# Two phases of attention scores cut anew, with one query tile's scores in the output banks and the division ahead of the minima

## The chip, the cores and the metric

The kernel runs on one core of one Trainium2 chip. The metric is the device time of one execution in microseconds (us). Three runs of the kernel before took 685.50, 690.76 and 686.28 us, so the median is 686.28 us; one more, profiled execution took 683.86 us.

## The reference

A windowed attention over 8 batches and 8 heads is followed by a mixture of experts. Only the attention is touched by the change.

```python
B, H, S, D = (8, 8, 576, 64); window = 128
scores = scale * q @ k^T
mask = (rel >= 0) & (rel < window)          # rel = query position - key position
scores = where(mask, scores + slope[h] * -abs(rel), -1e9)
attn = exp(scores - max(scores)); attn = attn / (sum(attn) + 1e-9)
x = attn @ v                                # then x becomes 4608 tokens of 512
logits = x @ w_gate                         # each expert takes the 576 best tokens left
out[mask_e] = relu(x[mask_e] @ w1[e]) @ w2[e]
```

## The kernel before

**The work of a pair.** Two heads of one batch make a pair, so there are 32 pairs. A query tile `t` holds 128 queries, two blocks of 64, of one head (`t` = 0 to 3), and a fifth half tile holds the remaining block of both heads. Which block remains depends on the parity of the batch: in even batches `t` = 0 has 2 key blocks and `t` = 4 has 3, in odd batches `t` = 0 has 3 and `t` = 4 has 1; tiles 1 to 3 always have 3. A key block is 64 columns wide. All of it is in fp32 on 64x64 quadrants of TensorE (PE), four products at a time: two heads by two query blocks.

**The steps of a pair**, each on one engine:

- `scores` (PE, through `mm`, L54): products of queries and keys into two banks `s`, one for each head, of 512 columns.
- `least` (VectorE, DVE, L134): bias and score are added, and the smallest value of each row goes to `mn`. Tiles 0 to 3 take one instruction for each head, the half tile takes two.
- `exps` (ScalarE, ACT, L145): the exponential, with the row's sum.
- `turn` (PE, L158 and L54): the weights are transposed into banks `pt`; `turned` (L166) copies them out, tiles 2 and 0 on ACT, tiles 1 and 3 on DVE.
- `av` (PE): products of values and weights into two banks `x`; `copy_out` (ACT, L214) copies them to `xT`.
- `natural` (PE): `xT` is transposed back and multiplied by the gate's weights, into two `pt` banks `N`.
- `divide` (DVE, L240 to L255): the reciprocal of the row sums, then the gate's part `Lp` and the output `xb` of both `N` banks are multiplied by it; `store` sends `xb` out on the DMA queue of SP.

**Banks.** PSUM has eight banks: `ps_s` has 2, `ps_t` (tiles `pt`) has 4 and `ps_x` has 2. `scores` is called twice for a pair, with `UNITS = (2, 3), (0, 1, 4)` (L23), and takes two tiles of `ps_s` each time, so the second half can be written only when the minima of the first half have read the same two banks.

**The order.** The loop over `n` (L316) writes the work of several pairs into one pass, and `put` (L51) keeps each engine to the order in which the code is written. In a pass the order is: `copy_out` of pair n-4, `least` of pair n-1's second half, `turn` of pair n-2's tiles 2, 1 and 3, `exps` of the second half, the copies of `pt`, `natural` of pair n-4, `turn` of tiles 0 and 4, at most one step of the router's early work on DVE (`router.early_step`), `scores`, `least` and `exps` of pair n's first half, `divide` of pair n-4, `av` of pair n-3, and `scores` of pair n's second half. Each of these engines runs its own instructions in that order and waits where another has not come so far.

## Time and profile before

| what | value |
|---|---|
| median of 3 runs | 686.28 us (685.50 to 690.76) |
| the profiled execution | 683.86 us, span 681.7 us |
| PE busy | 655.0 us, 96% of the span |
| DVE busy | 468.5 us, 69% |
| ACT busy | 386.4 us, 57% |
| attention's passes with scores | to about 204 us of the span |
| routing and experts | the rest of the span |

The profile lists, for each group of instructions, its busy time, the mean of one and the idle time of the engine ahead of them with what ended it. A busy PE is not a PE at its peak: the ends of products are modelled, and a product that overlaps others counts as busy. The timeline gives the start of each instruction or run of equal instructions in us, its length, the engine, the line and the tiles, and in brackets the idle time ahead of it. The engines wait for one another through semaphores.

### The profile page before, as it was taken

The numbers are of one execution on the slowest core, as the hardware profiler recorded it, in microseconds if no ns is written. First come the engines' busy times: TensorE is split into PE (matmuls) and PEld (weight loads), VectorE is DVE, ScalarE is ACT, GpSimd is POOL, SyncE is SP. The second block draws the span as 40 slices with busy tenths as digits, with TensorE's granted clock in tenths as the row PEclk, the third lists the DMA queues.
The fourth block names the chain that finished last, engine by engine and source line by source line (L and its number), as shares of the span: only waits on it lengthen the run. The fifth ranks groups of instructions, "written<-read, shape, count | busy, mean of one in ns | idle before, by whom it ended". The sixth has DMA issues, their size and how long they took to land.

```text
span 681.7 us, 18901 instructions
## 1 busy us (share of the span) xinstructions
PE 655.0 (96%) x7152; PEld 580.3 (85%) x7152; DVE 468.5 (69%) x1985; ACT 386.4 (57%) x1091; POOL 134.2 (20%) x296
## 2 busy tenths in 40 slices
PE   7999999999996699999999999999999999999995
PEld 4998998998986399889779879989989989989985
DVE  5788888888887799979749879776756625423210
ACT  6998898898884162434224546455546645644210
POOL 4021121121121201421412124013014014011011
PEclk9999999999998699999999999999999999999999
DMA  8556566566532361814515736637546556421001
GB/s 304 155 180 203 180 181 205 178 185 201 179 101 76 99 220 53 295 39 155 178 47 198 191 115 214 130 100 228 111 116 201 137 119 201 124 70 39 1 25 50
DMA packets 58980, 98.65 MB, mean 145 GB/s; under 512 B 27648, under 2 KB 36992, under 8 KB 58880
## 3 DMA queue, kind: packets, MB, share of 16 engines
q1 hardware_dynamic: 52992, 78.48, 38.6%
q0 software_dynamic: 5888, 18.88, 8.4%
q8 instruction: 58, 0.95, 0.6%
q14 instruction: 42, 0.34, 0.2%
HBM read 72.57 MB, written 18.87 MB: 134 GB/s over the span
## 4 chain that ended last, share of the span: by engine, by line
PE 86%; DVE 8%; DMA 3%; issue 1%; ACT 1%; POOL 0%; SPq 0%; POOLq 0%; DVEq 0%; ACTq 0%
PE ph L1059 24%; PE po L1087 10%; PE po L1088 10%; PE s L54 9%; PE po L1090 8%; PE pt L54 7%; PE pt L158 7%; PE x L54 6%; DMA raw<-in_w_dram 2%; DVE hl L967 2%; DVE hlo L1069 1%; PE m L610 1%; DVE u L134 1%; PE pg L1000 1%; PE ph L984 1%
## 5 line engine op out<-in xcount | busy, mean ns | idle before, releaser
L1059 PE MATMUL ph<-xh,hl 128*128 128x288 f32 (+2 forms) x1024 | 188.3, 298 | 0.6 <-ACT hh L1064 0.5
L1059 PEld LDWEIGHTS ph<-xh,hl 128*128 128x128 f32 x1024 | 154.6, 189 | 2.1 <-ACT hh L1064 0.7
L145 ACT ACTIVATE u<-u,mn 128x192 f32<-128x192 f32 (+2 forms) x288 | 123.9, 433 | 24.5 <-DVE mn L134 24.5
L1087 PE MATMUL po<-hl,hh 128*128 128x512 f32 (+1 forms) x328 | 128.3, 391 | 0.0
L1088 PE MATMUL po<-hl,hh 128*128 128x512 f32 (+1 forms) x328 | 126.2, 385 | 0.0
L1059 PE MATMUL ph<-xl,hl 128*128 128x288 f32 (+2 forms) x512 | 115.5, 297 | 0.0
L134 DVE CUSTOM_DVE_ANT_0 u<-s,bm 128x192 f32<-128x192 f32 x308 | 86.5, 333 | 30.0 <-PE s L54 29.2
L1064 ACT ACTIVATE hh<-ph 128x288 fp32r<-128x288 f32 (+2 forms) x128 | 46.5, 408 | 106.3 <-PE ph L1059 103.1
L1090 PE MATMUL po<-hl,hlo 128*128 128x512 f32 (+1 forms) x264 | 101.3, 384 | 0.0
L967 DVE TENSOR_TENSOR hl<-raw,hl 128x512 fp32r<-128x512 f32 x128 | 85.1, 684 | 22.0 <-ACT hl L965 21.6
L1099 POOL DMA_INDIRECT out_dram<-o,idx x40 | 42.2, 1056 | 274.9 <-ACT o L1094 216.0
L1059 PEld LDWEIGHTS ph<-xl,hl 128*128 128x128 f32 x512 | 84.1, 189 | 0.2 <-DVE xl L1038 0.2
L965 ACT CAST hl<-raw 128x1024 fp32r<-128x1024 f32 x64 | 65.9, 1051 | 22.1 <-DMA raw<-in_w_dram 17.7
L54 PE MATMUL s<-qk 64*64 64x192 f32 (+1 forms) x1112 | 69.7, 319 | 1.9 <-DVE mn L134 1.6
L1069 DVE SCALAR_TENSOR_TENSOR hlo<-ph,hh 128x288 fp32r<-128x288 f32 (+2 forms) x128 | 49.1, 416 | 32.5 <-ACT hh L1064 31.9
L1087 PEld LDWEIGHTS po<-hl,hh 128*128 128x128 f32 x328 | 61.8, 188 | 11.2
L1088 PEld LDWEIGHTS po<-hl,hh 128*128 128x128 f32 x328 | 61.7, 188 | 11.3
L1094 ACT COPY o<-po 128x512 f32<-128x512 f32 (+1 forms) x33 | 18.9, 573 | 91.0 <-PE po L1090 80.8
L1090 PEld LDWEIGHTS po<-hl,hlo 128*128 128x128 f32 x264 | 49.7, 188 | 9.9
L158 PE MATMUL pt<-ident_sb,u 128*128 128x128 f32 x368 | 54.2, 282 | 1.4 <-DVE mn L134 1.0
L54 PEld LDWEIGHTS s<-qk 64*64 64x64 f32 x1112 | 48.3, 132 | 8.1 <-issue 2.5
L145 ACT ACTIVATION_READ_ACCUMULATOR u<-u,mn 128x1 f32 x288 | 54.4, 189 | 0.0
(240 smaller groups left out, 902.6 us busy)
## 6 DMA issues: line engine op xcount, KB each, us to landing
raw<-in_w_dram SPq DMA_DIRECT2D x64, 512.0 KB, 4.3
qk<-in_qk_dram SPq DMA_DIRECT2D x32, 576.0 KB, 5.1
v<-in_v_dram SPq DMA_DIRECT2D x32, 288.0 KB, 3.6
x<-xb SPq DMA_DIRECT2D x14, 512.0 KB, 3.5
x<-xb SPq DMA_DIRECT2D x8, 128.0 KB, 3.2
x<-xb SPq DMA_DIRECT2D x4, 256.0 KB, 2.3
g<-x,idx POOLq DMA_INDIRECT x40, 3.8
out_dram<-o,idx POOLq DMA_INDIRECT x40, 2.8
```

The source lines that it names most:

```text
L54: put(nc.tensor.matmul(out, w, a, start=start, stop=stop, skip_group_check=True))
L134: put(nc.vector.tensor_tensor_reduce(out=u[rows], in0=x[rows, c:c + 64 * m].rearrange("q (j k) -> q j k", k=64), in1=bm[n % NP][rows, y:y ...
L145: put(nc.scalar.activation(u, u, AF.Exp, bias=st["mn"][:, i:i + 1], scale=-1.0, accum_out=st["sm"][:, i:i + 1]))
L158: put(nc.tensor.transpose(ps[:, c:c + 128], u[:, o + 128 * j:o + 128 * j + 128], ident))
L965: self.last = nc.scalar.copy(hl[:, 0, :], raw)
L967: nc.vector.tensor_tensor(hl[:, 1, c:c + 512], raw[:, c:c + 512], hl[:, 0, c:c + 512].bitcast(F32), ALU.subtract)
L1059: nc.tensor.matmul(pp[t], w[:, a, j, fo:fo + 128], x[:, j, cut[t]:cut[t + 1]], start=(i == 0), stop=(i == 11))
L1064: self.acted = nc.scalar.activation(o, pp[t], AF.Relu)
L1069: nc.vector.scalar_tensor_tensor(d, pp[t][:, c0:c1], 0.0, o[:, c0:c1].bitcast(F32), ALU.max, ALU.subtract)
L1087: nc.tensor.matmul(out, a, wh, start=(f == 0), stop=False)
L1088: nc.tensor.matmul(out, a, wl, start=False, stop=(f == 7 and t == 4))
L1090: nc.tensor.matmul(out, hl[:, f, 128 * t:128 * t + 128], wh, start=False, stop=(f == 7))
```

## The change

The two halves of a pair's scores become a large and a small part. `units(n)` gives tiles 2, 1, 3 and 0 (even batches) or 4 (odd batches) to the first part, and the tile that is left, 4 or 0, to the last. Both parts write the same two `s` tiles, which are now taken once for a pair. Tile 1's scores go to columns 320 to 511 of the first and 256 to 447 of the second of two new `x` tiles, `st["spare"]`; the same tiles are then the output banks of `av(k - 1, ...)`, which writes their columns 0 to 319 and 0 to 255. The last part's tile goes where tile 2's scores were.

The minima and exponentials are cut in another place than the scores: `part(n, 0)` is tiles 2 and 1, `part(n, 1)` is tile 3 and the two others. So four minima follow the first part, and six follow the last one, as before. `divide` (with its stores, and `logits` behind it) moves ahead of the four minima in the pass.

```diff
+    def units(n):
+        return (2, 1, 3, 4 * (n // NP % 2)), (4 - 4 * (n // NP % 2),)
+
+    def place_of(n, t, h):
+        st = state[n]
+        if t == 1:
+            return st["spare"][h], 320 - 64 * h
+        return st["s"][h], 192 * (t - 2) if t in (2, 3) else 384 if t in units(n)[0] else 0
...
-    def scores(n, half):
+    def scores(n, last):
...
-        s = [bank() if half and n < 2 else ps_s.tile([128, 512], F32, name="s") for _ in range(2)]
-        for t in UNITS[half]:
...
+            st["s"] = [ps_s.tile([128, 512], F32, name="s") for _ in range(2)]
+            st["spare"] = [ps_x.tile([128, 512], F32, name="x") for _ in range(2)]
+        for t in units(n)[last]:
...
+    def part(n, second):
+        first, last = units(n)
+        return first[2:] + last if second else first[:2]
...
-    def av(n):
+    def av(n, x=None):
...
-        x = st["x"] = [ps_s.tile([128, 512], F32, name="s") if n == NPAIRS - 1 else ps_x.tile([128, 512], F32, name="x")
-                       for _ in range(2)]
+        if x is None:
+            x = [ps_s.tile([128, 512], F32, name="s") if n == NPAIRS - 1 else ps_x.tile([128, 512], F32, name="x")
+                 for _ in range(2)]
+        st["x"] = x
...
             scores(n, 0)
-            least(n, 0)
-            exps(n, 0)
         if ends:
             divide(k - 2, N)
             if (k - 2) % NP == NP - 1 and k - 2 < NPAIRS - 1:
                 logits((k - 2) // NP)
+        if n < NPAIRS:
+            least(n, 0)
+            exps(n, 0)
         if 0 <= k - 1 < NPAIRS - 1:
-            av(k - 1)
+            av(k - 1, state[n]["spare"] if n < NPAIRS else None)
```

How this moves the instructions is shown at three places of a pass in an even batch. A row names line, operation and tiles, then in brackets the engines' semaphores that the instruction waits for (DVE_49 is VectorE's, PE_49 TensorE's, DMAHW the DMA queues').

The first place is PE, from the first scores of a pair to the start of `av`. Before:

```order
L54 MATMUL s<-qk 64x192 [waits DMAHW6_49]
L54 MATMUL s<-qk 64x192 x7
L54 MATMUL x<-PT_1031,v 64x128 [waits DMAHW3_49]
L54 MATMUL x<-PT_1031,v 64x128
L54 MATMUL x<-PT_1014,v 64x64 x2
```

The same place after the change:

```order
L53 MATMUL s<-qk 64x192 [waits DMAHW2_49]
L53 MATMUL s<-qk 64x192 x3
L53 MATMUL x<-qk 64x192 x4
L53 MATMUL s<-qk 64x192 x4
L53 MATMUL s<-qk 64x128 x4
L53 MATMUL x<-PT_1156,v 64x128 [waits DMAHW5_49,DVE_49]
L53 MATMUL x<-PT_1156,v 64x128
L53 MATMUL x<-PT_1139,v 64x64 [waits DVE_49]
```

Fourteen or sixteen products stand ahead of `av` where eight stood, and the first product into each `x` bank now waits for DVE. The counts it waits for are those that the minima of tile 1 raise, of the same pair whose scores stand just ahead: the third of the four minima for the first bank, the fourth for the second.

The second place is PE from the end of `av` to the next pass. Before:

```order
L54 MATMUL x<-PT_1016,v 64x64 x2
L54 MATMUL s<-qk 64x128 [waits DVE_49,PE_49] x2
L54 MATMUL s<-qk 64x128 x2
L54 MATMUL s<-qk 64x192 x6
L158 MATMUL pt<-ident_sb,u 128x128 x3
```

The same place after the change:

```order
L53 MATMUL x<-PT_1156,v 64x64 x2
L53 MATMUL x<-PT_1141,v 64x64 x2
L53 MATMUL s<-qk 64x192 x2
L172 MATMUL pt<-ident_sb,u 128x128 [waits PE_49]
L172 MATMUL pt<-ident_sb,u 128x128 x2
```

Ten products that waited for DVE, for the third and fourth minima, have become two (four in odd batches) that wait for nothing of their own.

The third place is DVE, around the division. Before:

```order
L134 ISA u,mn<-s,bm_304 128x3x64
L134 ISA mn 128x1
L240 RECIPROCAL rs<-sd 128x10 [waits Pool_49]
L248 TENSOR_TENSOR Lp<-pt,rs 128x3x2x8 [waits DVE_49]
L255 TENSOR_TENSOR xb<-pt,rs 128x3x128
L248 TENSOR_TENSOR Lp<-pt,rs 128x2x2x8
L255 TENSOR_TENSOR xb<-pt,rs 128x2x128
L134 ISA u,mn<-s,bm_304 128x3x64 [waits PE_49]
```

The same place after the change:

```order
L180 COPY PT_870<-pt 128x384 [waits PE_49]
L256 RECIPROCAL rs<-sd 128x10 [waits Pool_49]
L264 TENSOR_TENSOR Lp<-pt,rs 128x3x2x8 [waits DVE_49,PE_49]
L271 TENSOR_TENSOR xb<-pt,rs 128x3x128
L264 TENSOR_TENSOR Lp<-pt,rs 128x2x2x8 [waits PE_49]
L271 TENSOR_TENSOR xb<-pt,rs 128x2x128
L148 ISA u,mn<-s,bm_304 128x3x64 [waits PE_49,Activation_49]
L148 ISA mn 128x1
L148 ISA u,mn<-s,bm_304 128x3x64 [waits PE_49]
```

The division stood between the four minima and the six; it now stands between the copies of `pt` and the four minima. The first minimum waits for the last product of the first part into its `s` bank (that of tile 0 or 4), and the first of the six, which reads tile 3, waits for the last part's product into that bank.

## The prediction

> **What bounds the kernel now.** I read the page's groups, then the waits in attention, then the timeline of one pass engine by engine, and last a table of stretches. The page's groups put almost all idle time of DVE ahead of the minima, ended by PE's scores, and on PE a little ahead of the scores, ended by minima:

> ```profile
> L134 DVE CUSTOM_DVE_ANT_0 u<-s,bm 128x192 f32<-128x192 f32 x308 | 86.5, 333 | 30.0 <-PE s L54 29.2
> L54 PE MATMUL s<-qk 64*64 64x192 f32 (+1 forms) x1112 | 69.7, 319 | 1.9 <-DVE mn L134 1.6
> ```

> So each waits for the other, and the pass is a ring. The timeline of DVE in one pass (even batch, no router step) shows its part of it:

> ```profile
> 160.09 0.36 DVE L134 CUSTOM_DVE_ANT_0 u<-s,bm 128x192 f32<-128x192 f32 x1 [0.79 <-PE s L54]
> ...
> 161.20 0.21 DVE L240 RECIPROCAL rs<-sd 128x10 f32<-128x10 f32 x1
> 162.14 0.41 DVE L255 TENSOR_TENSOR xb<-pt,rs 128x256 f32<-128x256 f32 x1
> 162.47 0.28 DVE L134 CUSTOM_DVE_ANT_0 u<-s,bm 128x128 f32<-128x128 f32 x1
> 164.21 1.02 DVE L166 COPY PT<-pt 128x384 f32<-128x384 f32 x2
> 166.58 0.36 DVE L134 CUSTOM_DVE_ANT_0 u<-s,bm 128x192 f32<-128x192 f32 x1 [1.35 <-PE s L54]
> ...
> 167.42 0.35 DVE L134 CUSTOM_DVE_ANT_0 u<-s,bm 128x192 f32<-128x192 f32 x1
> 167.69 0.08 DVE L134 DVE_READ_ACCUMULATOR2_ANT mn<- 128x1 f32 x1
> 167.69 0.21 DVE L240 RECIPROCAL rs<-sd 128x10 f32<-128x10 f32 x1
> ```

> The columns are start, length, engine and line. From 166.58 on stand four minima (1.11 to the reciprocal), and behind 161.20 the division (1.27 to the next minimum), six minima (1.74), two copies (1.02) and 1.35 idle. The timeline of PE in the same pass:

> ```profile
> 162.46 1.20 PE L158 MATMUL pt<-ident_sb,u 128*128 128x128 f32 x9
> 163.49 1.39 PE L54 MATMUL pt<-wn_sb,xT 128*128 128x144 f32 x10
> 164.82 0.44 PE L158 MATMUL pt<-ident_sb,u 128*128 128x128 f32 x2
> 165.47 0.38 PE L54 MATMUL s<-qk 64*64 64x192 f32 x2
> 165.59 0.82 PE L54 MATMUL s<-qk 64*64 64x192 f32 x14
> 166.18 1.57 PE L54 MATMUL x<-PT,v 64*64 64x64 f32 x64
> 167.65 1.37 PE L54 MATMUL s<-qk 64*64 64x128 f32 x20
> 168.95 0.33 PE L158 MATMUL pt<-ident_sb,u 128*128 128x128 f32 x1
> ```

> Here `turn`'s tiles, `natural`, tile 0 (164.82), the first scores (165.47, ending 166.41), `av` (166.18) and the second scores (167.65) follow each other. PE looks full, but two starts are set by DVE: tile 0 goes into a `pt` bank that the first copy frees and starts 0.61 behind it (164.21 to 164.82), and the second scores start 1.07 behind the first minimum (166.58 to 167.65). The ring is: four minima 1.11, division 1.27, six minima 1.74, copy to tile 0 0.61, to the scores 0.65, scores 0.94, to the first minimum 0.17: 6.49. The table of stretches has the same for whole passes; the columns are stretch, length, busy time of PE, PEld, DVE, ACT and POOL, clock and DMA:

> ```profile
> 161.20:167.69 6.49, 6.49 (x136) 5.76 (x135) 5.06 (x28) 5.53 (x23) 0.94 (x5) 1.00 0.61 189
> 167.69:174.19 6.50, 6.50 (x140) 5.78 (x139) 5.07 (x28) 5.54 (x23) 0.94 (x5) 1.00 0.57 173
> 129.56:135.92 6.36, 6.36 (x141) 5.86 (x139) 5.35 (x32) 5.54 (x23) 0.94 (x5) 1.00 0.61 186
> 135.92:142.15 6.23, 6.23 (x135) 5.73 (x132) 4.93 (x28) 5.54 (x23) 0.94 (x5) 1.00 0.60 156
> ```

> The first two rows are even batches, the fourth an odd one, 0.27 shorter; mean of the four 6.40.

> **The change, part by part.** No arithmetic is added or left out, so the sum is the ring drawn anew.

> *What leaves the ring.* The division now stands on DVE in front of the four minima, where 1.35 was idle: 1.27 leaves. The wait of the second scores goes too. They last 1.30 (167.65 to 168.95), of which three groups stream 0.21+0.32+0.32 (the first scores are two groups of four products in the four quadrants and take 0.71 to the start of `av`, less some 0.07 to begin with; 128 columns take two thirds of 192), and I put 0.09 for the change of tiling, so 0.36 was wait.

> *What enters: a wait at `av`.* Its first product into each `x` bank now waits for a minimum of the scores written just before. Behind it are queued on PE the rest of `av`, the last scores and the next pass; for it wait ACT's copy to `xT` and, through the last scores, all six minima. The trace has no such wait at `av`; the nearest row is the second scores' own, which waited for the third minimum in the same way: 1.07 after the first. The second bank waits for the fourth, 0.27 later (167.42 to 167.69); bounds 0 and 0.27, I take 0.25, since the order runs through both banks in turn and only the first two products are ahead. `av` itself takes 1.47 (166.18 to 167.65).

> *The six minima come late.* The last part begins when `av` ends; one group takes 0.62 to its end (0.94 less the other group's 0.32), and 0.17 later DVE may start: 0.79. From the first minimum to the six it was 1.11+1.27 = 2.38; it becomes 1.07+0.25+1.47+0.79 = 3.58: +1.20. The copy of tile 1 and with it tile 0 are behind the six minima as before, so this reaches the next scores in full. On PE alone, tile 0 could start at its end of `natural`; it was hardly later (163.49+1.39 = 164.88 to 164.82), and now PE waits there some 0.4.

> *A longer first part.* One more group of 192 columns (0.32) and tile 0's of 128 (0.21) or tile 4's of 64 (0.11) come ahead of the first minimum, less 0.05 for the shorter last product: +0.46 on average, since the minimum waits for the last product into its bank, not for its own tile.

> *The division's cover.* From the first copy, PE's way to the first minimum is now 0.61+0.65+0.94+0.17+0.5 = 2.87; DVE needs 1.02 for the copies and 1.27 for the division, 2.29. A router step makes it longer:

> ```profile
> 152.31 0.21 DVE L452 TENSOR_REDUCE b<-L_sb 128x4 f32<-128x32 f32 x1
> ...
> 152.78 0.19 DVE L452 SCALAR_TENSOR_TENSOR cand<-ne,c_eb 128x32 bf16<-128x32 bf16 x1
> ```

> That is 0.66 in one pass of four (2.95) and some 0.42 in another (2.71), against 2.6 to 2.9: +0.06 on average. ACT has 5.5 busy of 6.4 and of 8.1 afterwards, and nothing of it is on the ring. POOL's queue keeps its order; on SP's a few loads of `v` change places with `qk` and stores, two passes ahead of their use, and the stores leave with the division, which nothing on the ring reads: nothing.

> *The sum.* 1.20+0.46+0.06 = 1.72 for a pass. The steady passes lie between the first minima of pairs 3 and 31:

> ```profile
> 20.19 0.35 DVE L134 CUSTOM_DVE_ANT_0 u<-s,bm 128x192 f32<-128x192 f32 x1
> ...
> 199.34 0.36 DVE L134 CUSTOM_DVE_ANT_0 u<-s,bm 128x192 f32<-128x192 f32 x1
> ```

> 28 passes in 179.15, 6.40 each: +48 us. At the start, the first two pairs' second scores lay in `pt` banks and the minima ran without a gap:

> ```profile
> 6.96 0.36 DVE L134 CUSTOM_DVE_ANT_0 u<-s,bm 128x192 f32<-128x192 f32 x1
> ...
> 12.31 0.36 DVE L134 CUSTOM_DVE_ANT_0 u<-pt,bm 64x192 f32<-64x192 f32 x1
> ```

> Now pair 1's scores wait for all minima of pair 0 (1.4 with their streaming), and four pairs pay about 0.5 for the longer first part and 0.5 for the last: +5 (bounds 2 and 8). Behind the last pair the six minima are late once more, +1. Together +54 us: 683.86+54 = 738 for the profiled execution, which lay 2.4 under the median, so 740 for the median.

> [...] The order shows that `av` waits though it writes other columns than the minima read. [...]

> **The rivals.**

> 1. *Faster: the waits go by columns.* If `av` and the six minima did not wait for other columns of a bank, the ring would be gone and PE's own work would decide: 6.40 less the 0.36 of wait, 28 times, is -10: 676. It decides if the third minimum is over when the first part ends. Against it are the order's waits, and that the minima cannot begin before the first part's end.
> 2. *No change: the change doesn't do what it says.* The old wait of 0.36 goes and the new one is met by then: 686. It needs the scores to end 1.3 before `av` is due; nothing in the rows gives that.
> 3. *Only `av` waits.* If tile 0 does not wait for the late copy, a pass grows by PE's waits alone: (0.17+0.32 end of the scores, less 0.07, plus 1.07+0.25) 1.74, less 0.36 and tile 0's 0.1: 1.28, so 36+6: 728. For it: the copy is only some 0.4 late.
> 4. *DVE becomes the bound.* If the division ends 0.3 behind the first scores in every pass, not in one of four, +8: 748.
> 5. *The clock falls.* In routing it fell behind a long gap of PE:

> ```profile
> 217.94 0.63 PE L452 MATMUL m<-OH,ind 128*128 128x16 bf16 x5 [3.09 <-DVE ind L452]
> ...
> 214.00:217.00 3.00, 0.85 (x7) 0.63 (x6) 2.62 (x15) 2.33 (x13) 0.00 (x0) 1.00 0.29 87
> 217.00:220.00 3.00, 0.69 (x6) 0.40 (x6) 2.37 (x17) 0.95 (x5) 0.00 (x0) 0.59 0.48 131
> ```

>    The granted clock went from 1.00 to 0.59 and on to half. At half clock PE's 6.0 of a pass would be 12, with 1.7 of wait 13.7: +7.3, 28 times, 890. Against it: the new gap is about 1.7, and PE stays busy for three quarters of a pass. [...]

> **How the numbers follow.** The forecast has 0.74: its steps are rows of the trace, put in the order that the built program has. Rival 3 has 0.12, rival 4 0.06, the faster one 0.03, no change 0.02, the clock 0.03. The forecast's own bounds are 0.15 a pass (4 us), 3 at the start and the runs' own spread of some 3: 731 to 747. With rivals 3 and 4 the range is 726 to 750. Slower by over 1% (about what a measurement can tell from no change) has 0.95, within 1% 0.02, faster 0.03.

> **What would show it.** In the profile after, passes of 7.9 to 8.3; DVE's idle time ahead of the four minima under 0.7 and a new idle stretch of over 1 us ahead of the six; PE idle some 1.4 ahead of `av`, ended by the minima; tile 0 again 0.61 behind the first copy; the granted clock 1.00 in attention, and routing and experts unchanged in length. It is wrong if `av` starts right behind the scores, if passes stay near 6.4, or if the experts' part grows.

## The result, and the profile after

| | before | after |
|---|---|---|
| median of 4 runs | 685.89 us | 726.13 us (725.43 to 728.64) |
| ratio, 95% interval | | 1.0578 (1.0522 to 1.0634) |
| span of the profiled execution | 681.7 us | 723.6 us |

The changed kernel is slower by 40 us, where 54 were forecast; the forecast of 740 (726 to 750) was too high. The kernel was measured once more beside the experiments below, with a ratio of 1.0547 (1.0516 to 1.0579).

The page's busy line and its groups show the two waits between VectorE and TensorE in their new places (last columns: idle time ahead of the group, and what ended it):

```profile
PE 660.1 (91%) x7151; PEld 577.3 (80%) x7152; DVE 470.1 (65%) x1985; ACT 389.4 (54%) x1091; POOL 134.8 (19%) x296
...
L148 DVE CUSTOM_DVE_ANT_0 u<-s,bm 128x192 f32<-128x192 f32 (+3 forms) x256 | 73.5, 329 | 65.1 <-PE s L53 63.8
...
L53 PE MATMUL x<-PT,v 64*64 64x64 f32 (+1 forms) x2048 | 57.7, 250 | 35.4 <-DVE mn L148 35.4
...
L53 PE MATMUL s<-qk 64*64 64x192 f32 (+2 forms) x896 | 63.7, 315 | 2.9 <-DVE mn L148 2.9
```

VectorE's idle time ahead of the minima was 30.0 and is 65.1. `av`, ahead of which TensorE had no such wait, now has 35.4 of it, all ended by minima: 35.4 over the 29 calls of `av` that share their banks with scores is 1.22 each, and that is nearly the growth of a pass.

The timeline of TensorE in one pass of an even batch without a router step (start, length, engine, line, shape; the idle time ahead in brackets):

```profile
74.61 1.72 PE L53 MATMUL x<-PT,v 64*64 64x128 f32 x60 [1.15 <-DVE mn L148]
76.08 0.33 PE L53 MATMUL s<-qk 64*64 64x192 f32 x2
...
76.50 1.20 PE L172 MATMUL pt<-ident_sb,u 128*128 128x128 f32 x9
77.54 1.39 PE L53 MATMUL pt<-wn_sb,xT 128*128 128x144 f32 x10
78.96 0.44 PE L172 MATMUL pt<-ident_sb,u 128*128 128x128 f32 x2
```

and VectorE's in the same pass:

```profile
73.64 0.36 DVE L148 CUSTOM_DVE_ANT_0 u<-s,bm 128x192 f32<-128x192 f32 x1 [0.45 <-PE s L53]
73.92 0.35 DVE L148 CUSTOM_DVE_ANT_0 u<-s,bm 128x192 f32<-128x192 f32 x1
74.20 0.35 DVE L148 CUSTOM_DVE_ANT_0 u<-x,bm 128x192 f32<-128x192 f32 x1
74.48 0.35 DVE L148 CUSTOM_DVE_ANT_0 u<-x,bm 128x192 f32<-128x192 f32 x1
76.60 0.36 DVE L148 CUSTOM_DVE_ANT_0 u<-s,bm 128x192 f32<-128x192 f32 x1 [1.76 <-PE s L53]
...
78.35 1.02 DVE L180 COPY PT<-pt 128x384 f32<-128x384 f32 x2
79.40 0.22 DVE L256 RECIPROCAL rs<-sd 128x10 f32<-128x10 f32 x1
...
81.27 0.36 DVE L148 CUSTOM_DVE_ANT_0 u<-s,bm 128x192 f32<-128x192 f32 x1 [0.45 <-PE s L53]
```

`av` starts 74.61-73.64 = 0.97 behind the first minimum, that is as the third minimum ends, and TensorE is idle for 1.15 until then. The six minima start at 76.60, behind the last part of the scores, 2.96 after the first minimum instead of 2.38. Tile 0 (78.96) starts 0.61 behind the first copy (78.35), as it did before. The pass takes 81.27-73.64 = 7.63; its kind took 6.49.

By the same anchors as in the prediction, the 41.9 by which the span grew lie here:

| stretch | before | after | growth |
|---|---|---|---|
| to pair 3's first minimum | 20.19 | 20.81 | 0.6 |
| 28 passes, to pair 31's | 179.15 | 214.46 | 35.3 |
| from there to routing's first count | 18.60 | 20.93 | 2.3 |
| from there to the end | 463.8 | 467.4 | 3.6 |

### The profile page after: what moved, and what is told of

It reads as the page before. It is cut to its first block, busy times and chain, and to the rows that moved or that the text cites. A ratio compares the mean times of both kernels' runs of the same rounds, so it can differ in the third digit from the quotient of the medians.

```text
span 723.6 us, 18867 instructions
## 1 busy us (share of the span) xinstructions
PE 660.1 (91%) x7151; PEld 577.3 (80%) x7152; DVE 470.1 (65%) x1985; ACT 389.4 (54%) x1091; POOL 134.8 (19%) x296
## 4 chain that ended last, share of the span: by engine, by line
PE 76%; DVE 18%; issue 2%; another core or an unknown queue 1%; DMA 1%; ACT 1%; POOL 0%; POOLq 0%; SPq 0%; DVEq 0%
PE ph L1076 25%; PE po L1104 10%; PE po L1105 9%; PE x L53 8%; PE po L1107 7%; DVE u L148 7%; PE pt L53 4%; PE pt L172 4%; PE s L53 4%; DVE PT L180 2%; DVE xb L271 2%; PE ph L1001 1%; DVE hl L984 1%; PE pg L1017 1%
## 5 line engine op out<-in xcount | busy, mean ns | idle before, releaser
L148 DVE CUSTOM_DVE_ANT_0 u<-s,bm 128x192 f32<-128x192 f32 (+3 forms) x256 | 73.5, 329 | 65.1 <-PE s L53 63.8
L53 PE MATMUL x<-PT,v 64*64 64x64 f32 (+1 forms) x2048 | 57.7, 250 | 35.4 <-DVE mn L148 35.4
L53 PEld LDWEIGHTS x<-PT,v 64*64 64x64 f32 x2048 | 51.0, 136 | 43.1 <-DVE mn L148 40.7
L53 PE MATMUL s<-qk 64*64 64x192 f32 (+2 forms) x896 | 63.7, 315 | 2.9 <-DVE mn L148 2.9
```

Source lines behind the costliest of these rows:

```text
L53: put(nc.tensor.matmul(out, w, a, start=start, stop=stop, skip_group_check=True))
L148: put(nc.vector.tensor_tensor_reduce(out=u[rows], in0=x[rows, c:c + 64 * m].rearrange("q (j k) -> q j k", k=64), in1=bm[n % NP][rows, y:y ...
```

## The experiments

Two theories came from the trace, and one from the diff. **A**: the loss is TensorE's wait at `av` for tile 1's minima. **B**: it is the ring of the forecast, in which the six minima come late because the last part of the scores stands behind `av`. **C**: the division is in the wrong place. The kernel before ran beside each of three groups of experiments: 683.52 us beside the division behind, the division ahead, the last part ahead and tile 1 first; 683.14 beside six minima first, both other places of the division, and the router's step; 686.24 beside the changed kernel once more and the last experiment. The expectations of the first group and of the router's step start from 685.9 for the kernel before, so their measurements are best read by the ratio, times 685.9.

For the passes the following table gives what their timelines show: the medians of the 11 even and 11 odd passes between pairs 5 and 27, from the first minimum to the second group of minima, from there to the first copy, and on to tile 0, to the first scores and to the next first minimum.

| kernel | first to second group | to copy | to tile 0 | to scores | to first | even pass | odd pass |
|---|---|---|---|---|---|---|---|
| before | 2.38 | 1.74 | 0.61 | 0.66 | 1.10 | 6.49 | 6.24 |
| changed | 2.96 | 1.75 | 0.61 | 0.66 | 1.65 | 7.63 | 7.47 |
| division behind | 2.96 | 1.75 | 0.61 | 0.66 | 1.65 | 7.63 | 7.46 |
| last part ahead | 1.12 | 2.53 | 0.02 | 1.94 | 1.65 | 7.25 | 7.00 |
| tile 1 first | 2.40 | 1.75 | 0.61 | 0.65 | 1.13 | 6.54 | 6.79 |
| six minima first | 2.40 | 1.20 | 1.31 | 0.60 | 0.78 | 6.29 | 6.25 |
| division in the middle | 3.37 | 1.26 | 1.17 | 0.60 | 0.78 | 7.18 | 7.07 |
| division in halves | 2.53 | 1.26 | 1.17 | 0.60 | 0.78 | 6.35 | 6.24 |

The columns between the name and the last two are those of even batches. In the row "last part ahead" tile 0 doesn't wait for the copy, so its 0.02 is the next transpose of another tile, and 1.94 holds the rest of the way.

**The changed kernel once more**, without an edit, to have it beside the others.

> The changed kernel as it is, beside the same runs of the kernel before as the other experiments. Its profiled execution took 467.5 from the first routing count to the end, the kernel before 463.8, the other experiments 462.2 to 465.3 with the same code there. If the 3.6 us are an execution's own: 462 to 465 here, and a ratio of 1.052 to 1.055, so that putting the division back or moving the router is worth 2 to 4 us less than it seemed. If they belong to the change: 467 again and a ratio of 1.058.

Measured: 723.15 us, ratio 1.0547 (1.0516 to 1.0579). From the first routing count to the end it took 465.3, not 467.5; the passes are the same to 0.01. The profiles of all other kernels here, with the same code in that part, have 462.2 to 465.3 there. So it isn't shown that the 3.6 of the first table belong to the change; more than half of them were that execution's own. A part of that can be seen: in the first profile the granted clock was at half once more in that part, from 420.6 to 424.1 us of the span, and its mean over the span was 0.982 where the second had 0.983; 3.4 us at half clock can cost up to 1.7, as an estimate. In what follows experiments are compared with 1.0547.

**Division behind the four minima again** (theory C):

```diff
-        if ends:
-            divide(k - 2, N)
-            ...
         if n < NPAIRS:
             least(n, 0)
             exps(n, 0)
+        if ends:
+            divide(k - 2, N)
+            ...
```

> The changed kernel with the division put back behind the four minima; the new places of the scores and all else stay. Theory A (the loss is TensorE's wait at av for tile 1's minima): the division fits into VectorE's idle stretch ahead of the six minima (2.96 from the first minimum to the six, less 1.11 of minima, is 1.85, and the division takes 1.42), so it costs nothing there; only the passes with a router step gain 0.1 to 0.2, the last two pairs more: 720 to 726 us. Theory C (the division ahead of the minima is what costs): 1.3 a pass come back, 28 passes, 690 us.

Measured: 717.76 us, ratio 1.050 (1.0478 to 1.0521). Passes without a router step are the same to 0.01: the division only takes another of VectorE's two idle stretches. C falls, and A's 720 to 726 holds (1.050 times 685.9 is 720). The 3 us gained on 1.0547 lie elsewhere: beside the second profile of the changed kernel the 28 passes are 2.1 shorter, 1.5 of it in the four behind pair 27, where the division had stood behind router steps, and the stretch behind pair 31 is 1.5 shorter, of which the last section tells.

**Division ahead, alone**, in the kernel before:

```diff
             scores(n, 0)
-            least(n, 0)
-            exps(n, 0)
         if ends:
             divide(k - 2, N)
             ...
+        if n < NPAIRS:
+            least(n, 0)
+            exps(n, 0)
```

> The kernel before with the division moved ahead of the four minima, and nothing else. Theory A: the division fills 1.35 of idle time, but the second scores still wait 1.07 for the third minimum and take 1.30, and 0.17 later the six minima start, 2.54 behind the first instead of 2.38: 0.0 to +0.2 a pass, and +0.2 in each of 8 passes with a router step: 686 to 693 us, the ring only changes hands. Theory C: the first minima come late in every pass, 700 us or more. A reading in which the division in the ring is what bounds the kernel before: -1 a pass, 660 us.

Measured: 692.43 us, ratio 1.0113 (1.0077 to 1.015). That is 694 of 685.9, just over A's 686 to 693 and far from the others: passes without router steps are 6.40 (even) and 6.28 (odd) instead of 6.49 and 6.23, those with router steps up to 0.7 longer, where A had 0.2, and the last one 1.1. Taking 1.27 out of the ring gained nearly nothing, since the six minima still wait for the second scores and come only 0.13 earlier behind the first minimum (2.25 instead of 2.38, even). Through the router steps the 28 passes are 7.1 longer in all. 3.8 more of the profile's growth lie ahead of pair 3; the last section comes back to them.

**The last part ahead of `av`** (A against B):

```diff
+        if n < NPAIRS:
+            scores(n, 1)
         if 0 <= k - 1 < NPAIRS - 1:
             av(k - 1, state[n]["spare"] if n < NPAIRS else None)
...
-        if n < NPAIRS:
-            scores(n, 1)
```

> The changed kernel with the last part of the scores written ahead of av instead of behind it, so that it runs while av would wait, and the six minima no longer stand behind av. It waits for the first two minima, so it starts 0.64 behind the first minimum and av starts 1.06 behind it (now 0.98). Theory A: TensorE's own path from the first minimum to the turn of tile 2 becomes 0.64+0.42+1.50 = 2.56 instead of 2.86, and the early copy gains little more, since natural ends only just ahead of the copy as it is: 0.2 to 0.3 a pass, 717 to 721 us. Theory B (the loss is the six minima's lateness behind av): they start 1.2 instead of 2.96 behind the first, and 0.5 a pass or more come back: 712 us or less.

Measured: 707.66 us, ratio 1.0353 (1.033 to 1.0376). TensorE's timeline in an even pass:

```profile
71.77 0.81 PE L53 MATMUL s<-qk 64*64 64x192 f32 x4 [0.59 <-DVE mn L148]
72.33 1.83 PE L53 MATMUL x<-PT,v 64*64 64x128 f32 x64
74.09 1.20 PE L172 MATMUL pt<-ident_sb,u 128*128 128x128 f32 x9
75.13 1.39 PE L53 MATMUL pt<-wn_sb,xT 128*128 128x144 f32 x10
76.36 0.38 PE L172 MATMUL pt<-ident_sb,u 128*128 128x128 f32 x2
```

and VectorE's:

```profile
71.35 0.36 DVE L148 CUSTOM_DVE_ANT_0 u<-s,bm 128x192 f32<-128x192 f32 x1 [1.13 <-PE s L53]
...
72.47 0.35 DVE L148 CUSTOM_DVE_ANT_0 u<-s,bm 128x192 f32<-128x192 f32 x1
...
75.00 1.02 DVE L180 COPY PT<-pt 128x384 f32<-128x384 f32 x2 [0.82 <-PE pt L172]
```

The time is on B's side, the place is mostly not. The six minima now follow at once (72.47, 1.12 behind the first), 1.84 earlier, but a pass gains only 0.38. The first copy is ended by TensorE's transposes (0.82), so the ring is open. From first minimum to tile 2's turn TensorE takes 74.09-71.35 = 2.74 instead of 76.50-73.64 = 2.86, from there to tile 0 2.27 instead of 2.46: only these 0.19 are the copy's lateness, B's part. The other 0.19 are TensorE's own path and its effect on the first minimum. In the changed kernel both paths end together: `natural` ended at 77.54+1.39 = 78.93, and tile 0, held by the copy, started at 78.96. A had the place and too small a gain; more of it lies in the odd passes (0.47 each) and at the end (2.1 between pairs 27 and 31, 2.0 behind them).

**Tile 1 first**, in the scores and in the minima:

```diff
-        return (2, 1, 3, 4 * (n // NP % 2)), (4 - 4 * (n // NP % 2),)
+        return (1, 2, 3, 4 * (n // NP % 2)), (4 - 4 * (n // NP % 2),)
```

> The changed kernel with tile 1 ahead of tile 2, in the first part of the scores and in the four minima, so that the minima that av waits for are the first two and wait for no product of the s banks. Theory A: av's wait falls from 1.4 to 0.2 to 0.4 (the division ends about 2.4 behind the first copy, the second minimum 0.54 later), and passes are 6.5 to 6.7: 689 to 695 us. Theory B: the six minima still stand behind av and the last part, 2.6 behind the first minimum instead of 2.96: -0.4 a pass, 715 us. Theory C: the division still stands ahead, 726 us.

Measured: 695.77 us, ratio 1.0167 (1.014 to 1.0194). Its groups:

```profile
L148 DVE CUSTOM_DVE_ANT_0 u<-s,bm 128x192 f32<-128x192 f32 (+3 forms) x256 | 73.4, 329 | 40.8 <-PE s L53 39.8
...
L53 PE MATMUL x<-PT,v 64*64 64x64 f32 (+1 forms) x2048 | 56.4, 246 | 11.4 <-DVE mn L148 10.8
```

One swap in a list brings back 26 us (0.038 of 684), two thirds of the loss: the wait at `av` falls from 35.4 to 11.4, since it now takes the first minimum (0.41 behind its start) and that one waits only for tile 1's own scores, in banks of their own. The ratio makes 697 of 685.9: near A's 695, its odd passes being 6.79 for a forecast of 6.7 at most, and 18 us and more from B's and C's. The six minima come earlier too (2.40), because all behind `av` does. That is 0.56 of the 1.09 that an even pass gains; most of the rest is the first minimum, which no longer waits for the end of the first part (1.13 behind the first scores instead of 1.65).

**Six minima first**, in the kernel with tile 1 first: `part` gives tiles 1, 2 and 3 to the first group.

```diff
-        return first[2:] + last if second else first[:2]
+        return first[3:] + last if second else first[:3]
```

> As the kernel with tile 1 first, and tile 3's minima and exponentials moved from the second group to the first: six minima before the last part, four behind it. The work behind the last part in the ring gets 0.55 shorter (six minima 1.75, four 1.2). If the ring through the late minima still decided with tile 1 first (first to second group 2.4, minima 1.75, copy to tile 0 0.61, to the scores 0.65, to the first minimum 1.13): 0.4 a pass or more come back, 684 us or less at 683.5 of the kernel before. If TensorE's own path decides by then: 0.1 to 0.2 a pass, 690 to 693 us.

Measured: 686.53 us, ratio 1.0052 (1.0022 to 1.0082). Here the ring did decide once more: with four minima behind the last part instead of six, tile 0 no longer waits for the copy (1.31 behind it), and a pass gains 0.25 (even) and 0.54 (odd). The expectation for "the ring decides" was 684 or less and for "TensorE decides" 690 to 693; the measurement lies between, since the ring decided until TensorE's own work did.

**Division in the middle**, in the kernel with six minima first: it stands behind tile 1's two minima:

```diff
+        return (first[:1], first[1:3], first[3:] + last)[k]
...
+            least(n, 0)
+            exps(n, 0)
+        if ends:
+            divide(k - 2, N)
+            ...
+            least(n, 1)
+            exps(n, 1)
```

> As the kernel with six minima first, with the whole division behind tile 1's two minima instead of ahead of them. TensorE's wait at av is then gone, since the first minima can start while the rest of the first part still streams; but VectorE has the copies, two minima, division 1.42, four and four minima behind one another with an idle stretch ahead of the first minimum, about 6.4 a pass: 684 to 690 us. If av still waits, the wait has another cause than the division: 690 us or more.

Measured: 706.98 us, ratio 1.0338 (1.0305 to 1.0371), a miss by 17 us and more. The wait at `av` is gone, as expected, and a new one stands behind it:

```profile
86.88 1.83 PE L53 MATMUL x<-PT,v 64*64 64x128 f32 x68
89.24 0.83 PE L53 MATMUL s<-qk 64*64 64x192 f32 x8 [0.54 <-DVE mn L148]
```

The last part is written over tile 2's columns, in the same two banks as tile 3's, and so waits for the minima of both, and both now stand behind the division, which takes 1.26 from its start to tile 2's first minimum. The expectation had counted VectorE's work and left this wait out.

**Division in halves**, again in the kernel with six minima first: the reciprocal and the first `natural` bank ahead of tile 1's minima, the second bank behind them, with `divide` a generator that yields in between.

```diff
-        for i in range(2):
-            shares(i)
-            ...
+        shares(0)
+        ...
+        yield
+        shares(1)
```

> As the kernel with six minima first, with the division cut in two: reciprocal and the first natural bank ahead of tile 1's two minima (0.9, which fits into the 1.0 between the copies and tile 1's scores), the second bank behind them (0.5). Neither av nor the last four minima should wait then, and TensorE's own work decides: turn and natural 2.4, tile 0 0.6, first part 1.2 to 1.35, av 1.47, last part 0.42 to 0.58, 6.15 to 6.35 a pass, against 6.37 before: 679 to 686 us. If the ring still decides, 690 us or more.

Measured: 684.77 us, ratio 1.001 (0.9989 to 1.003): no wait of TensorE is listed between 40 and 190 us, the time is in the 679 to 686 that were expected without waits, and it is the old one. So with the same places for the scores nearly all of the loss is gone once no product waits for a minimum. What the 23 passes between pairs 4 and 27 gain (6.32 instead of 6.37, 1.2 us), the start (1.0) and the four passes behind them (1.6) take back.

**The router's step at the end of the pass**, in the changed kernel:

```diff
-            if ends:
-                router.early_step(room)
             scores(n, 0)
...
         if n < NPAIRS:
             scores(n, 1)
+            if ends:
+                router.early_step(room)
```

> The changed kernel with the router's early step written at the end of a pass, behind the last part of the scores, instead of ahead of the scores, so that it runs on VectorE while it waits for the last part and no longer delays division and minima. If the forecast's term for the division's cover (0.06 a pass) was too small because of router steps: seven passes gain about 0.17 each, the passes of pairs 30 and 31 0.5 and 1.3, and TensorE's wait of 2.05 at the last av becomes about 1.0, which also shows whether the lower clock there (0.72 in 235 to 241) belongs to that wait: 4 to 6 us less than the changed kernel, ratio to the kernel before 1.049 to 1.053. If router steps are covered: no difference, 1.058.

Measured: 717.06 us, ratio 1.0482 (1.0448 to 1.0516), 4.5 us better than 1.0547. The 4 to 6 us were expected, but they have another reason: the 28 passes gain only 1.0, since in some the router's work now delays the copies. 2.0 are gained behind pair 31's first minimum, where the lower clock is missing (last section), and 2.5 lie in the part that varies by itself.

**Both together**, the division in halves and the router at the end:

> The kernel with the division in halves, and the router's early step at the end of the pass, where VectorE waits 0.65 for the last part anyway. The passes of pairs 30 and 31, 7.25 and 7.93 against 6.58 and 6.83 in the kernel before, should lose 0.5 to 1.0 together, seven passes 0.05 each; start-up keeps its 1.0 over the kernel before: 682.5 to 684 us at 683.1 of the kernel before, ratio 0.998 to 1.001. If the router's products now hold TensorE back, 685 us or more.

Measured: 684.08 us beside 686.24, ratio 0.9963 (0.9945 to 0.9981). It is the one version that beats the kernel before, by 0.4%, a little more than the 0.998 to 1.001 that were expected: the passes of pairs 30 and 31 are 6.45 and 7.14, 1.6 shorter together. Its stretch of 32 us, after a row of the kernel before (columns as in the prediction):

```profile
136.00:168.00 32.00, 31.88 (x649) 28.72 (x650) 26.16 (x143) 27.92 (x113) 5.94 (x29) 1.00 0.62 193
```

```profile
136.00:168.00 32.00, 32.00 (x691) 28.98 (x687) 27.26 (x146) 28.15 (x115) 5.94 (x29) 1.00 0.59 195
```

TensorE counts as busy throughout in both. In this order of work, with almost no wait left, 0.07 a pass (6.30 against 6.37) is what the new scores gave.

## Why the prediction was right in kind and too high

**Right, and shown.** `av` waits for tile 1's minima: it starts at the third minimum's end, 0.97 behind the first, in all passes, and when tile 1's place shortens that wait and frees the first minimum from the first part's end, two thirds of the loss go. In passes without router steps the division's place costs and gains next to nothing (0.00 to 0.09 in both of its experiments); with router steps ahead of it, it costs. The old wait moved to a place with more work queued behind it, as the forecast had it. Tile 0 starts 0.61 behind the copy, as forecast, so rival 3, whose 728 is nearest to the result, is not right in its mechanism; but it was right that TensorE's own path is as long. Its 1.28 a pass has the same 1.07 and 0.25 in it as the forecast, so that it meets the measured 1.26 is partly luck. The clock did not fall in the 28 passes (rival 5): it was 1.00 from the first record at 4.22 us to 236.33, at the last `av` (last section). Rivals 1, 2 and 4 did not come. `av` waits though it writes other columns than the minima read, 1.12 to 2.05 in each of the 29 calls (1.15 in the pass above); no run here leaves that wait out of the order.

**Where it failed: the sum for a pass, 1.72 where the passes between pairs 4 and 31 measure 7.66 instead of 6.40, 1.26.** Nearly all of it is in "the six minima come late", which was put at 3.58 from first minimum to six and measures 2.96 (even) and 3.19 (odd):

- *The second bank's wait, 0.25: nearly nothing.* The last part starts 1.46 to 1.51 behind `av`'s start, as the second scores did in the kernel before (1.47). The forecast had added the two waits one behind the other. The first product into the second bank does start 0.28 behind `av`'s first product, but without a wait (division in halves, even passes) it starts 0.17 behind, so it is held for 0.11 only; `av`'s last product is 0.10 later (1.61 instead of 1.51) and the last part 0.03 (1.46 instead of 1.43). The lower bound of 0 was nearly right.
- *From the last part to the six minima, 0.79: 0.52 (76.08 to 76.60) in even batches, 0.70 in odd.* The forecast took one group's length from the first scores, whose groups have four products; in even batches the last part has two (76.08 in the timeline above starts them). That this is the reason is argued, not tried.
- *The restart at `av`, 1.07: 0.97.*

Together 0.25+0.27+0.10 are the 0.62 of the even pass; in odd ones 0.39. The longer first part was sized well: +0.55 (1.10 to 1.65) and +0.40 for a forecast of +0.46.

**The smaller terms.** The start was put at +5 and is +0.6 (0.9 in the second profile): the first minimum comes 0.3 earlier in the first profile alone (6.66; 6.97 in the second, 6.96 before), the first pass grows by 1.7, but the next two, whose waits were there before too, get 0.2 and 0.6 shorter. The division's cover, 0.06 a pass, holds on the middle passes (7.59 with router steps, 7.55 without), but not at the end, where four and seven router operations stand ahead of the division: the four passes from pair 27 grew by 6.1 instead of some 5. Behind the last pair +1 was forecast and 2.3 came; with the router moved, where the clock stayed up, it is 0.25. The 3.6 in routing and experts were forecast as none; the second profile has 1.5, and 0.0 is within what executions differ by.

So 48 for the passes was 35, 5 for the start was 0.6, 1 for the tail was 2.3. The signs, the waits and the places held. What the range lacked was a bound for the sum of three waits that were each taken near their upper ends: the lower bound of 0 that the prediction itself gave the second bank, 7 us over 28 passes, did not enter it (and its bounds of 4, 3 and 3 add up to 10 either way, not to the 9 and 7 of 731 to 747).

**Not settled.** The wait of 0.36 that the forecast took out of the second scores of the kernel before was not tried by itself. That a pass without any wait is only 0.07 shorter speaks for less, but there the scores are also cut and placed otherwise.

## What to carry to other kernels

A buffer that is lent to a second user brings its release along: write down for each wait what must be finished, how late that is in its engine's order, and what stands behind the waiting instruction. Here the same sharing costs 5.5% with tile 1 third and fourth in the minima and 1.7% with it first and second, by one swap in a list, and 0.1% with the division in halves. Other work on the reading engine counts where a wait hangs on the reads behind it: ahead of or behind all four minima the division made some 0.5% (1.0547 and 1.050), between the minima in the last part's way 2.9% (1.0338 against 1.0052). And when a wait sits on two paths of nearly equal length, undoing the longer one alone shows only their difference, so take both before judging the change.

## What was not expected of the hardware

**The clock fell behind 2.05 us of waiting.** At the last `av` with scores ahead of it TensorE waited longest, for the seven router operations and the division. The timeline's row and stretches of half a microsecond (PE's busy time after the length; the clock is third from the end):

```profile
236.23 2.89 PE L53 MATMUL x<-PT,v 64*64 64x128 f32 x60 [2.05 <-DVE mn L148]
```

```profile
235.50:236.00 0.50, 0.00 (x0) 0.00 (x0) 0.50 (x5) 0.28 (x1) 0.42 (x2) 1.00 0.00 0
236.00:236.50 0.50, 0.27 (x4) 0.24 (x4) 0.46 (x4) 0.50 (x3) 0.42 (x2) 0.82 0.41 137
236.50:237.00 0.50, 0.50 (x15) 0.49 (x15) 0.00 (x0) 0.50 (x4) 0.42 (x3) 0.50 1.04 344
...
239.00:239.50 0.50, 0.50 (x16) 0.36 (x9) 0.00 (x0) 0.24 (x1) 0.00 (x0) 0.50 0.00 0
239.50:240.00 0.50, 0.50 (x8) 0.15 (x2) 0.03 (x1) 0.46 (x2) 0.00 (x0) 0.76 0.00 0
```

The clock was at half for some 3.4 us, from about 236.3 to 239.75, and the last part came 2.57 behind `av`'s start instead of 1.51. Both profiles of the changed kernel have it at this place, the second from 236.5 to 239.9. With the router moved, the same `av` waited 1.12 and the clock stayed at 1.00:

```profile
235.43 1.72 PE L53 MATMUL x<-PT,v 64*64 64x128 f32 x60 [1.12 <-DVE mn L148]
```

The waits of 1.12 to 1.46 in the other passes never lowered it. A gap of 2.05 was enough here; the gap in which the clock fell in routing, in the kernel before, was 3.09.

The traces show how long the clock stays at one value. From the first record to the last change, the stretches of full and of half clock in this profile last 232.11, 3.41, 17.07, 17.07, 146.77, 3.41 and 296.96 us, which is 68, 1, 5, 5, 43, 1 and 87 times 3.413. In the kernel before they last 211.63, 17.07 and 443.73: 62, 5 and 130 times. In the ten other profiles the stretches between two changes up to 284 us are within 0.02 us of 1, 3, 4, 5, 60 and 66 times, from 3.42 to 225.28. The whole gap of 2.05 falls into the 3.42 us ahead of the change, in which TensorE was busy for 1.37:

```profile
232.91:236.33 3.42, 1.37 (x31) 1.18 (x32) 3.18 (x19) 0.96 (x4) 1.51 (x7) 1.00 0.01 4
236.33:239.74 3.41, 3.41 (x72) 3.00 (x72) 0.13 (x2) 1.73 (x8) 0.67 (x3) 0.50 0.63 195
```

**It also fell at the start, in some executions.** In the profile of the division ahead, alone, the clock was at half from 13.4 to 23.6 us, behind gaps on TensorE of 0.40 and 0.96; the kernel before has the same two gaps and kept 1.00. Most of that profile's 3.8 ahead of pair 3 lies in this stretch, and its four runs spread from 689.4 to 695.9. The division in the middle has it from 13.3 to 16.7, behind gaps of 1.02, 0.43 and 1.01; the kernel with six minima first has the same three and kept 1.00. So in these pairs the longest gap alone does not decide. The pieces ahead of these two falls had 0.60 and 0.58, where both happened; the kernel before had 0.60 and 0.58 at 9.3 and 12.7 us and stayed up. What decided these two falls was not shown.
